# Products of zeros ahead of the first q and k, and a longer placing distance for attention's work on TensorE

## The chip, the cores and the metric

The kernel runs on one core of a Trainium2 chip. The metric is the device time of one execution in microseconds (us). Each kernel was run several times, with runs of the kernel before in between on the same chip. The engines are PE (TensorE; PEld is its weight load), DVE (VectorE), ACT (ScalarE), POOL (GpSimd, which here also issues most loads) and SP (SyncE).

## The reference

Cosine attention for 8 batches, 12 heads, 448 tokens and head size 64, then a mixer: a low-rank sum over tokens (rank 32) and an MLP of 768 to 3072 to 768.

```python
q_n = q / (np.linalg.norm(q, axis=-1, keepdims=True) + 1e-06)
k_n = k / (np.linalg.norm(k, axis=-1, keepdims=True) + 1e-06)
scores = np.matmul(q_n, k_n.transpose(0, 1, 3, 2)) / tau
... softmax ...; x = attn @ v, heads side by side: (8, 448, 768)
h = x.transpose(0, 2, 1) @ U @ V            # sums over tokens
u = x + h.transpose(0, 2, 1)
out = u + np.maximum(u @ w_ch1, 0.0) @ w_ch2
```

## The kernel before

The kernel first writes down all its instructions as entries of a plan, each with an engine, an estimated duration and what it depends on. A small list scheduler then walks through planned time and fixes the order on each engine. On the chip each engine executes its instructions in that order and waits on semaphores where the plan was too optimistic. So the planned times decide only the order.

For PE there are several streams, and at each moment the first stream in the list whose head is ready gets its turn: transposes, then batch 0's scores, then attention times v, then U and V, then scores, and MLP last. MLP products thus fill what attention leaves. When an entry is ready is decided here:

```python
def ready_at(self, op, eng):                       # cut
    for d in op.deps:
        ...
        t = max(t, d.end + self.SEM + (self.SAFE if eng == "PE" else 0.0))   # SEM 0.10, SAFE 0.25
    ...                                             # the same for a buffer that must come free
```

The product of attention's result with U is made of four matmuls, each for 32 columns of the array and with its own token tile; they are four entries of the plan, the last three with a nominal 0.01 us:

```python
for t in range(4):                                  # in stage0, for each range of columns
    o = plan.add(Op("PE", pe_t(c1 - c0) + 0.2 if t == 0 else 0.01,
        lambda ...: nc.tensor.matmul(out=mm.tile[R * t:R * (t + 1), 0:c1 - c0],
            lhsT=U_sb[:, par, t, :], rhs=X.tile[:, t, c0:c1], start=True, stop=True), ...),
        pe_a if c1 < C else pe_av)
```

And batch 0 makes its sums u twice, once more by tokens: six products with V in a row, among the first-layer products of its MLP, each needing one of three PSUM banks that a DVE addition frees:

```python
if b == 0 and f == 9:                               # in mlp, f counts first-layer tiles
    by_tokens(us, *state["first"])                  # six products, six additions
```

## Time and profile before

| | value |
|---|---|
| median time | 607.53 us (607.23 to 608.25, 4 runs) |
| span of the profiled run | 604.8 us |
| PE busy | 586.1 us, 97% |
| first transposes on PE | 7.92 us |
| PE is the limit from | about 32.6 us |

PE's busy share uses modelled ends: a matmul's shown end lies up to 0.16 us behind the moment at which the next could start. Holes are therefore better read from the distance of two starts. Without any wait a score of 448 columns is followed by the next start after 0.189 us, a product of 384 columns after 0.163, one of 512 after 0.216. In this document "excess" is the distance of starts beyond that. The lines of the profile before stand in the prediction. A line of it that begins with two times gives the start (us from the beginning of the span) and the length of a merged run of instructions, then engine, source line, operation, output<-inputs, shapes and count; in brackets stand the engine's idle time before it and what ended that. Line numbers of the changed kernel are mostly two higher than those of the kernel before: scores are L563 and L565, the products with U L640 and L642.

### The profile page before, as it was taken

The page shows a single profiled execution, that of the slowest core. Times are in us where ns is not written, and L with a number is a line of the kernel's source. Part 1 is how long each engine was busy: PE and PEld are TensorE (multiplying, and loading weights), DVE is VectorE, ACT ScalarE, POOL GpSimd, SP SyncE. Part 2 cuts the span into 40 slices and gives each one's busy share as a digit, 9 for nine tenths or more (in the row PEclk, how much of TensorE's full clock was granted, in tenths as well). Part 3 has the DMA queues.
Part 4 walks back from the last instruction along what each step waited for, and adds up shares of the span by engine and source line. Part 5 has one row for each costly group of instructions (what it writes and reads, how often), then busy time and mean ns, then how long its engine had stood idle before and what let it go on. Part 6 is the DMA issues. An engine that isn't in the chain of part 4 may idle for free.

```text
span 604.8 us, 11544 instructions
## 1 busy us (share of the span) xinstructions
PE 586.1 (97%) x4725; PEld 346.8 (57%) x4725; DVE 296.0 (49%) x714; ACT 279.5 (46%) x612; POOL 115.4 (19%) x177
## 2 busy tenths in 40 slices
PE   3899999999999999999999999999999999999997
PEld 1665666555555665666445665666545666654565
DVE  8979679989998987644711253015300210110011
ACT  6977652498782385317641077506442025014300
POOL 8246334071715326000500000000000000000000
PEclk9999999999999999999999999999999999999999
DMA  9999998999999999514902151030002110310021
GB/s 114 202 184 122 208 198 103 173 145 126 129 145 175 151 139 154 83 56 87 154 0 66 46 90 37 1 93 27 15 1 53 52 40 1 92 40 1 0 53 53
DMA packets 150164, 54.58 MB, mean 90 GB/s; under 512 B 115040, under 2 KB 150112, under 8 KB 150112
## 3 DMA queue, kind: packets, MB, share of 16 engines
q0 software_dynamic: 73344, 25.96, 38.6%
q1 hardware_dynamic: 76704, 27.86, 24.2%
q8 instruction: 37, 0.61, 0.4%
q14 instruction: 15, 0.12, 0.1%
q10 hardware_dynamic: 64, 0.02, 0.0%
HBM read 52.25 MB, written 11.01 MB: 105 GB/s over the span
## 4 chain that ended last, share of the span: by engine, by line
PE 92%; ACT 5%; DVE 2%; issue 0%; ACTq 0%
PE mm L785 36%; PE mm L751 35%; PE sc L563 9%; PE av L583 8%; ACT attn L568 3%; PE mm L675 1%; ACT qkT L815 1%; PE tp L365 1%; PE mm L640 1%; DVE ss L452 1%; PE sc L751 1%; DVE xn L527 0%; PE sc L675 0%; ACT uT L815 0%; DVE xn L820 0%
## 5 line engine op out<-in xcount | busy, mean ns | idle before, releaser
L751 PE MATMUL mm<-uT,w_sb 128*128 128x512 bf16 (+1 forms) x1134 | 236.1, 353 | 0.0
L785 PE MATMUL mm<-w_sb,relu 128*128 128x384 bf16 (+1 forms) x1368 | 233.8, 323 | 0.3 <-ACT uT L815 0.3
L568 ACT ACTIVATE attn<-sc 128x448 bf16<-128x448 f32 x336 | 161.0, 565 | 88.8 <-PE av L583 57.4
L785 PEld LDWEIGHTS <-relu 128*128 128x128 bf16 x1368 | 132.6, 98 | 86.7 <-issue 0.9
L751 PEld LDWEIGHTS <-w_sb 128*128 128x128 bf16 x1152 | 111.9, 98 | 101.1 <-issue 1.0
L774 ACT ACTIVATE relu<-mm 128x512 bf16<-128x512 f32 (+1 forms) x169 | 92.4, 547 | 149.2 <-PE mm L751 148.9
L794 DVE TENSOR_TENSOR O_sb<-mm,u_nat 128x384 f32<-128x384 f32 (+1 forms) x57 | 31.0, 547 | 227.1 <-PE mm L785 223.4
L563 PE MATMUL sc<-qkT 128*128 128x448 bf16 x336 | 103.4, 358 | 3.9 <-ACT attn L568 1.9
L583 PEld LDWEIGHTS <-attn 128*128 128x128 bf16 x1536 | 62.7, 98 | 16.0 <-DVE xn L527 0.8
L409 POOL DMA_DIRECT2D v_nat<-in_v_dram x98 | 63.2, 651 | 34.7 <-DMA w_sb<-in_moe_w_ch_dram 13.4
L583 PE MATMUL av<-v_nat,attn 128*128 128x65 bf16 x1536 | 66.6, 194 | 0.2 <-DVE X_sb L592 0.2
L452 DVE TENSOR_REDUCE ss<-sq 112x8 f32<-112x512 bf16 x96 | 63.0, 673 | 0.3
L527 DVE TENSOR_TENSOR xn<-qk_nat,inv 112x512 bf16<-112x512 bf16 (+1 forms) x97 | 62.5, 674 | 0.3
L563 PEld LDWEIGHTS <-qkT 128*128 128x128 bf16 x336 | 29.8, 98 | 24.2 <-issue 8.0
L387 POOL DMA_DIRECT2D qk_nat<-in_q_dram x25 | 17.9, 716 | 130.6 <-DVE xn L527 102.6
L592 DVE TENSOR_TENSOR X_sb<-av,rd 128x256 bf16<-128x256 f32 x96 | 40.0, 419 | 1.5
L590 DVE RECIPROCAL rd<-av 128x4 f32<-128x4 f32 x96 | 17.0, 179 | 38.2 <-PE av L583 36.7
L448 DVE TENSOR_TENSOR sq<-qk_nat 112x512 bf16<-112x512 bf16 x90 | 35.0, 408 | 0.2
L689 DVE TENSOR_TENSOR u_nat<-mm,X_sb 128x384 bf16<-128x384 f32 x36 | 19.1, 553 | 11.0 <-PE mm L675 10.8
L365 PE MATMUL tp<-ident,xn 112*128 112x112 bf16 x144 | 11.7, 226 | 10.0 <-DVE xn L527 9.5
L465 ACT ACTIVATE ln<-ss 112x32 f32<-112x32 f32 (+2 forms) x26 | 6.3, 241 | 32.7 <-DVE ss L452 32.5
L387 POOL DMA_DIRECT2D qk_nat<-in_k_dram x25 | 17.6, 703 | 5.8 <-DMA w_sb<-in_moe_w_ch_dram 5.8
(58 smaller groups left out, 160.8 us busy)
## 6 DMA issues: line engine op xcount, KB each, us to landing
qk_nat<-in_q_dram POOLq DMA_DIRECT2D x23, 224.0 KB, 5.2
qk_nat<-in_k_dram POOLq DMA_DIRECT2D x23, 224.0 KB, 6.4
w_sb<-in_moe_w_ch_dram POOLq DMA_DIRECT2D x4, 1152.0 KB, 14.3
w_sb<-in_moe_w_ch_dram POOLq DMA_DIRECT2D x8, 576.0 KB, 16.6
out_dram<-O_sb SPq DMA_DIRECT2D x15, 168.0 KB, 2.3
out_dram<-O_sb SPq DMA_DIRECT2D x16, 144.0 KB, 2.1
out_dram<-O_sb SPq DMA_DIRECT2D x16, 120.0 KB, 2.0
out_dram<-O_sb SPq DMA_DIRECT2D x16, 96.0 KB, 2.2
```

The lines of the kernel that those rows point to most:

```text
L387: ops = [load(lambda i=i, src=src: nc.gpsimd.dma_start(out=ld.tile[:, i, lo:lo + h1 - h0, :], in_=src[b, h0:h1].rearrange("h (s c) d -> s ...
L409: nc.gpsimd.dma_start(out=vb[p0:p0 + s1 - s0, hs, j, 0:D], in_=v[b, hs].rearrange("h (s c) d -> c s h d", c=SC)[c, s0:s1]),
L448: nc.vector.tensor_mul(y, x, x)
L452: lambda i=i, a0=a0, a1=a1, sq=sq: nc.vector.reduce_sum(ss.tile[:, i, a0:a1, :].rearrange("p h c -> p (h c)"), sq.tile[:, 0:a1 - a0, :].re ...
L527: nc.vector.tensor_mul(dst, src, sc)
L563: nc.tensor.matmul(out=sc.tile[:, 0:S], lhsT=kT[:, 128 * m:128 * (m + 1)], rhs=qkT.tile[:, 8:12, :].rearrange("p c s -> p (c s)"), start=T ...
L568: exps[m] = plan.add(Op("ACT", act_t(S), lambda sc=sc, m=m: nc.scalar.activation(out=attn.tile[:, m, off:off + S], in_=sc.tile[:, 0:S], fu ...
L583: nc.tensor.matmul(out=av.tile[:, t, 0:D + 1], lhsT=attn.tile[:, m, 128 * t:128 * (t + 1)], rhs=v_t[b % 2][:, h, j, 0:D + 1], start=(j == ...
L592: muls.append(plan.add(Op("DVE", dve_t(256), lambda av=av, rd=rd, h=h: nc.vector.tensor_mul(X.tile[:, :, h * D:(h + 1) * D], av.tile[:, :, ...
L751: o = plan.add(Op("PE", pe_t(n), lambda cc=cc: nc.tensor.matmul(out=mm.tile[:, 0:n], lhsT=w1_sb[:, cc, f * 128:(f + 1) * 128], rhs=uT.tile ...
L774: nc.scalar.activation(out=relu.tile[:, f, 0:n], in_=mm.tile[:, 0:n], func=AF.Relu)
L785: nc.tensor.matmul(out=mm.tile[:, 0:c1 - c0], lhsT=relu.tile[:, f, i * 128:(i + 1) * 128], rhs=w2_t[:, f, c0:c1], start=(f == 0), stop=(f ...
```

## The change

It has two parts. Fifty products of zeros run on PE while it waits for the first q and k, with the intent that its clock is already released when the transposes come. And from batch 1 on, the attention entries of PE are placed at a distance of 0.8 us in place of 0.25 behind what they read, so that MLP products go first where the plan was too tight.

```diff
-    SAFE = 0.25
+    safe = 0.25
...
-        op.seq = self.n
+        op.seq, op.safe = self.n, self.safe
...
-                t = max(t, d.end + self.SEM + (self.SAFE if eng == "PE" else 0.0))
+                t = max(t, d.end + self.SEM + (op.safe if eng == "PE" else 0.0))
...
-            t = max(t, f + (self.SEM + self.SAFE if eng == "PE" else self.SEM))
+            t = max(t, f + (self.SEM + op.safe if eng == "PE" else self.SEM))
...
+    warm = const.tile([128, 128], BF, name="warm")
...
+    pe_warm = plan.stream("PE")
...
+    warm_set = fill(lambda: nc.vector.memset(warm, 0.0), 30, prio=-9)
+    hot = Slot(r_mm, 50)
+    for _ in range(50):
+        plan.add(Op("PE", 0.11, lambda: nc.tensor.matmul(
+            out=hot.tile[:, 0:128], lhsT=warm, rhs=warm, start=True, stop=True),
+            deps=[warm_set], acq=[hot], rel=[hot]), pe_warm)
...
     after = last_mul[-1:]
+    plan.safe = 0.8
     state["first"] = prev["A"], prev["X"]
...
+    plan.safe = 0.25
     for b in range(B):
         mlp(b, *state[b])
```

More of the change, by code (lines that the diff above doesn't have):

```diff
@@ L41 @@
 class Op:
-    __slots__ = ("eng", "dur", "fn", "deps", "acq", "rel", "prio", "lat", "start", "end", "by", "seq", "fast")
+    __slots__ = ("eng", "dur", "fn", "deps", "acq", "rel", "prio", "lat", "start", "end", "by", "seq", "fast", "safe")
     def __init__(self, eng, dur, fn, deps=(), acq=(), rel=(), prio=0, lat=0.0, fast=False):
```

## The prediction

> **What bounds the kernel now.** I read the busy shares first, then the stretches of the span, then the chain of waits, then single waits on PE in order of time.
>
> The page's busy shares and chain, by engine:
>
> ```profile
> PE 586.1 (97%) x4725; PEld 346.8 (57%) x4725; DVE 296.0 (49%) x714; ACT 279.5 (46%) x612; POOL 115.4 (19%) x177
> ...
> PE 92%; ACT 5%; DVE 2%; issue 0%; ACTq 0%
> ```
>
> PE carries 92% of the chain that ended last. The other 8%, mostly ACT and DVE, must lie where PE is not yet the limit. The table of stretches says where (columns: length, then busy time of PE, PEld, DVE, ACT, POOL):
>
> ```profile
> 8.00:18.70 10.70, 8.73 (x67) 4.99 (x68) 9.91 (x25) 9.08 (x27) 7.08 (x11) 1.00 1.70 157
> 18.70:32.60 13.90, 11.67 (x169) 8.05 (x168) 12.78 (x40) 13.90 (x37) 5.27 (x8) 1.00 1.16 193
> 32.60:40.00 7.40, 7.39 (x111) 5.00 (x111) 5.47 (x16) 5.78 (x14) 3.03 (x5) 1.00 1.18 187
> 40.00:102.00 62.00, 59.90 (x584) 38.45 (x582) 49.77 (x119) 36.44 (x81) 27.17 (x40) 1.00 1.19 163
> 102.00:240.00 138.00, 137.48 (x1246) 81.44 (x1244) 123.84 (x298) 87.25 (x203) 54.24 (x82) 1.00 1.23 148
> ```
>
> From 8 to 18.7 us DVE is busy 93% (9.91 of 10.70). From 18.7 to 32.6 ACT is busy for all of its 13.90. Only from 32.6 us on is PE the limit, and from there the end of the program is PE's stream of work plus whatever holes are in it. The chain in order of time agrees: DVE pieces up to 14.6 us, a PE piece, ACT pieces up to 32.6, then PE.
>
> What PE waits for first, in the list of waits on PE:
>
> ```profile
> PE tp L365 <- DVE xn L527: 9.5, 4, 7.9
> PE sc L563 <- ACT attn L568: 1.9, 5, 0.6
> PE sc L563 <- ACT qkT L815: 0.7, 2, 0.5
> PE sc L563 <- ACT relu L774: 0.6, 1, 0.6
> ```
>
> The 7.9 us are the start: loads, sums of squares, norms, then the first transposes. The products of zeros go into this hole.
>
> **The clock.** The table's clock column says 1.00 everywhere, but the durations contradict it: a 448-column score lasts a median 554 ns (429 to 581) up to 18.7 us and 350 ns after it; a transpose of 112 columns lasts 301 against 212 ns. The trace's clock record has its entry of full speed only from 18.9 us on; what is not recorded is evidently shown as 1.00. The Trainium skill, page "TensorE: Matmul & The Clock Gate", Part 1, says that PE starts at half clock, that about 3.4 us of sustained activity releases it, and that a start-to-start distance is N/1.2 ns cold and N/2.4 + 2.5 ns warm. The trace agrees: cold scores start 0.36 to 0.37 us apart (17.48, 17.84, 18.21; N/1.2 gives 0.373), warm ones 0.19. Sparse work from 7.9 us on did not release it for 11 us.
>
> **The change, first part: a memset and 50 products.** The same page gives 128/1.2 = 107 ns for each product cold: 50 x 0.107 = 5.35 us, less if the clock is released on the way. The memset of the zeros goes first on DVE, whose first instruction starts at 0.92 us, so the products run from about 1.2 to at most 6.7 us, before the first transposes at 7.92. They hold one of three mm banks until then and collide with nothing. That is 5.4 us of PE work that costs nothing.
>
> The memset does cost a little. DVE is in memsets without a break from 2.19 us to the first squares at 4.88, which its last memset holds up. The page "VectorE: DVE Perf Modes", section "Zero memsets can be issued as uint32 (trn2)", says that a memset takes a cycle per element and that zeros can go as uint32; the trace shows it (xn: 112x512 uint32 in 0.48 us). The zeros are 64 such words per partition: by 36 words in 0.09 and 198 in 0.22, some 0.1 us. It delays the first squares by that: +0.1 us.
>
> What a warm PE saves before 18.9 us counts only where another engine then waits for PE. ACT's waits on PE between 9 and 20 us, in order of time:
>
> ```profile
> 9.75 1.22 ACT L815 COPY qkT<-tp 128x336 bf16<-128x336 bf16 x6 [0.17 <-PE tp L365]
> ...
> 15.57 1.03 ACT L815 COPY qkT<-tp 128x672 bf16<-128x672 bf16 x3 [0.33 <-PE tp L365]
> ...
> 18.08 1.42 ACT L568 ACTIVATE attn<-sc 128x448 bf16<-128x448 f32 x3 [0.46 <-PE sc L563]
> ```
>
> That sums to 0.96 us. Most isn't passed on: the gain of 0.17 and 0.33 meets squares at 16.87 that wait for q and k to land (16.79), and DVE, nearly full, still delivers its normalised tiles at 13.87 and 19.39. I count the 0.46 at 18.08, less a third for DVE's pace: -0.3. PE's own 3.45 us on the chain from 14.61 to 18.05 would shrink by half, but this is the same saving. Net of the memset: -0.2 us, if the clock stays released across the sparse stretch. The page's Part 4 says that transposes don't count as activity in the same way, and the products end over 3 us before the scores at 10.35; I give 65% that it stays.
>
> **The second part: distance 0.25 to 0.8.** The instructions of PE are ordered by a plan made when the program is built; it lets an attention instruction of PE be placed only after its input's planned end plus 0.10 plus this distance. Nothing is added or removed on the chip: MLP products move ahead of attention's by 0.55 us of planned time. What it can gain is the holes after 40 us in which PE, though MLP products were to be had, stood before an attention instruction. The page's idle time hides part of each hole, since the modelled end of a matmul reaches 0.16 us past the next one's possible start. Read from starts: three scores take 0.73 us when nothing waits, four 0.92.
>
> ```profile
> 47.98 0.54 PE L563 MATMUL sc<-qkT 128*128 128x448 bf16 x2 [0.46 <-ACT qkT L815]
> ...
> 58.96 0.54 PE L563 MATMUL sc<-qkT 128*128 128x448 bf16 x2 [0.58 <-ACT relu L774]
> ...
> 147.09 1.10 PE L563 MATMUL sc<-qkT 128*128 128x448 bf16 x3
> ...
> 181.22 1.42 PE L563 MATMUL sc<-qkT 128*128 128x448 bf16 x4
> ...
> 288.95 1.28 PE L563 MATMUL sc<-qkT 128*128 128x448 bf16 x3
> ```
>
> The sum: first scores after qkT copies 0.62 and 0.74; transposes at 77.25 0.31; scores that wait for a bank from the exponentials 0.10, 0.37, 0.50, 0.42 (at 226.6) and 0.55: together 3.6 us. The transposes of u and what follows, 98.9 to 101.05: 0.49 + 0.24 + 0.15 + 0.45 = 1.3. In all 4.9 us. All start-to-start excess after 40 us is 8.7; the rest is mostly the L640 products at every change of column group (0.2 each, some 12 times) and batch 0, which this distance doesn't touch. Single holes are 0.1 to 0.74, so 0.55 more would close them wholly or all but 0.2. I count 75% of the 3.6 (-2.7), 30% of the 1.3 (-0.4; its last part is an MLP product waiting for a bank, and MLP keeps 0.25), and +0.6 for new holes that a new order makes. Net -2.5.
>
> The end is safe: attention's last score starts at 426.4 us and from 430 on PE is without holes for 174 us of MLP, so later attention costs nothing there.
>
> Sum: 607.3 - 0.2 - 2.5 = 604.6; I take 604.5.
>
> **Rivals.** (1) Nothing: the holes move, since a wait was real and the new order waits elsewhere; the clock saves nothing, as ACT and DVE set the pace to 32.6. For it: ACT's full 13.90. Time 606.5 to 607.5. (2) Attention becomes the bound: three score banks with 0.55 us more on each turn are planned at about 0.63 us a score instead of 0.44, so MLP of a batch runs out before the next batch is ready. Against it: batch 4's 42 scores now take 22.7 us (267.9 to 290.6), 26.5 would do, and 130 first-layer products (28 us) of the running batch still lie behind it at 293.6; after batch 1, 72 second-layer products (11.9 us at 101.05) were in hand. For it: DVE is 90% busy from 102 to 240 (123.84 of 138). If it happens: 609 to 612. (3) Warm PE pulls the whole start forward, all 0.96 of ACT's waits, and every hole closes: 607.3 - 0.9 - 4.9 = 601.5.
>
> **Range and chances.** The largest gain worked out is 5.8 us, 1.0%; 2% is 12.1 us. So faster by over 2% needs something not in the profile (1%); slower by over 2% needs a starved PE (1%). The range runs from most holes closed, 602.0, to a slight gain lost in new holes, 606.8.
>
> **What would show it.** Right: scores at 300 to 350 ns instead of 554 before 18.9 us; ACT's waits of 0.33 and 0.46 gone, yet the time at which PE becomes the limit (now 32.6) earlier by under 0.5; the holes at the first scores of a batch and between scores below 0.2; excess after 40 us near 6 instead of 8.7. Wrong: that moment a microsecond or more earlier; new waits of PE on DVE or on u and uT between 90 and 300 us; scores still cold at 12 us.

## The result, and the profile after

The changed kernel took 606.24 us (605.35 to 606.55, 4 runs) against 607.53: ratio 0.9975, 95% interval 0.9957 to 0.9992. Ratios here and below are the mean time of one kernel's fast runs over that of the other's in the same rounds, so they aren't quite the ratio of the medians. In later rounds it took 605.28 against 606.77, ratio 0.9971. So the change wins about 1.5 us, a quarter of a per cent.

The page after, PE's busy line and the chain by engine:

```profile
PE 591.2 (98%) x4775; PEld 351.6 (58%) x4775; DVE 300.7 (50%) x723; ACT 277.7 (46%) x604; POOL 115.7 (19%) x177
...
PE 93%; ACT 3%; DVE 2%; POOL 1%; DMA 1%; issue 0%; ACTq 0%; POOLq 0%
```

The 50 additional instructions are the products of zeros. In the chain (ACTq and POOLq are the sequencers of these engines) POOL and DMA are new: in this run its start goes through loads. PE's waits, longest first:

```profile
PE tp L367 <- DVE xn L529: 3.9, 4, 2.2
PE sc L565 <- ACT attn L570: 1.7, 4, 0.6
PE mm L864 <- DVE warm L861: 1.0, 1, 1.0
PE tp L367 <- ACT qkT L817: 0.4, 1, 0.4
PE sc L565 <- ACT qkT L817: 0.3, 1, 0.3
```

The hole at the start is partly filled (9.5 became 3.9). Of the waits of scores, 0.7 us on the copies of qkT became 0.3, and the 0.6 us on a relu (L774 before) is gone. The table of stretches of the changed kernel (length; then busy PE, PEld, DVE, ACT, POOL with counts; granted clock; DMA share; GB/s):

```profile
5.00:8.00 3.00, 0.85 (x16) 0.67 (x14) 2.90 (x8) 1.29 (x5) 2.92 (x6) 1.00 1.19 145
8.00:18.70 10.70, 8.48 (x66) 4.85 (x66) 9.69 (x25) 8.88 (x26) 7.04 (x11) 0.52 1.71 159
18.70:32.60 13.90, 11.61 (x169) 8.04 (x168) 12.91 (x39) 13.90 (x38) 6.58 (x9) 1.00 1.22 202
```

The clock column of the second row is the surprise: 0.52 from 8 to 18.7 us. The trace's clock record shows full speed from 4.78 us, for 3.41 us, then half speed from 8.20 for 10.24 us, and full again from 18.43. (In all traces here such stretches are whole multiples of 3.41 us, except the last one of a run, which the trace cuts off; this unit is called a window below.) The products (first line below, start 1.0 to 5.5 us, 311 ns cold and 219 warm) did release the clock, but it was gone again before the first scores. Those are as slow as before (second line, the ten up to 18.7 us; before 429 to 581 with a median of 554, eleven of them):

```profile
L864 PE MATMUL mm<-warm x50: 219/311/312, 1.0 to 5.5; 128*128 128x128 bf16 x50
```

```profile
L565 PE MATMUL sc<-qkT x10: 373/544/581, 10.3 to 18.4; 128*128 128x448 bf16 x10
```

**Where the 1.25 us between the two profiled runs come from.** I took the trace's PE instructions in order and summed their excess. Up to 45 us PE had lost 19.86 us before and 20.02 after: +0.16. From 45 us to the last product it lost 7.40 before and 6.19 after: -1.21. The tail after the last product is 4.00 and 3.80. Sorted by kind, the excess over 0.04 us after 40 us, apart from the products with U, fell from 5.54 to 3.08 us:

| excess after 40 us, before what and released by whom | before | after |
|---|---|---|
| scores, by exponentials | 1.94 | 0.49 |
| first scores, by qkT copies or a relu | 1.41 | below 0.1 |
| transposes of u and the product after them | 1.33 | 0.11 |
| by-token products of batch 0 and the product after them | 0.47 | 1.58 |
| products with V, and attention times v | 0 | 0.42 |
| the first MLP products, by batch 0's own uT | 0.40 | 0.40 |

The first scores of batch 1, behind a hole of 0.62 us before (47.98 us in the prediction), now follow the product ahead of them without a wait:

```profile
50.51 0.73 PE L565 MATMUL sc<-qkT 128*128 128x448 bf16 x3
```

And of the four scores that took 1.42 us at 181.22 us in the kernel before, with two holes of about 0.25, the first two now have MLP products between them, and none of the four waits:

```profile
187.98 0.35 PE L565 MATMUL sc<-qkT 128*128 128x448 bf16 x1
188.16 1.14 PE L787 MATMUL mm<-w_sb,relu 128*128 128x384 bf16 x6
189.14 0.35 PE L565 MATMUL sc<-qkT 128*128 128x448 bf16 x1
```

The by-token row is the largest new hole. The products of the changed kernel in order of time:

```profile
49.50 1.17 PE L723 MATMUL mm<-A_sb,V_sb 128*128 128x384 bf16 x3
...
51.87 0.79 PE L723 MATMUL mm<-A_sb,V_sb 128*128 128x384 bf16 x2 [0.24 <-DVE u_nat L727]
...
53.40 0.81 PE L753 MATMUL mm<-uT,w_sb 128*128 128x384 bf16 x4 [0.19 <-DVE u_nat L727]
```

Three such products take 0.65 us without a wait (two distances of 0.163 and one length of 0.32); the first line shows 1.17. Before, scores stood in three of the five gaps between the six, now in two, and most of them wait for a bank.

And there is a loss in the products with U that I hadn't looked for. Before the change (first fence) and after it (second):

```profile
129.78 0.38 PE L751 MATMUL mm<-uT,w_sb 128*128 128x512 bf16 x1
130.09 0.35 PE L640 MATMUL mm<-X_sb,U_sb 128*32 128x384 bf16 x4
130.37 0.36 PE L563 MATMUL sc<-qkT 128*128 128x448 bf16 x1
```

```profile
134.39 0.34 PE L642 MATMUL mm<-X_sb,U_sb 128*32 128x384 bf16 x1
134.66 0.68 PE L585 MATMUL av<-v_nat,attn 128*128 128x65 bf16 x16
135.27 0.34 PE L642 MATMUL mm<-X_sb,U_sb 128*32 128x384 bf16 x3
135.54 0.74 PE L565 MATMUL sc<-qkT 128*128 128x448 bf16 x3
```

Four of them together hold PE for 130.37 - 130.09 = 0.28 us, and the first starts 0.31 us after the 512-column product before it, 0.09 later than that one's pace of 0.216. They use different columns of the array and run side by side, as the Trainium skill says in "TensorE: Matmul & The Clock Gate", Part 3 ("Packing small matmuls"). Split in one and three, each part holds PE for 0.27 us (134.66 - 134.39 and 135.54 - 135.27) and each pays the 0.09 in front. One split of this size so costs about 0.27 + 0.09 = 0.36 us, as much as a whole group. The changed kernel has four such splits after 40 us (at 78, 88, 134 and 169 us, of different widths), the kernel before none; both have one in batch 0.

The excess at these groups grew by 1.17 us. In the kernel before it still held a hole right behind one group, which the change closed: the transposes at 77.25 us start 0.54 us after that group's first product (76.71), and a whole group of 512 columns holds PE for 0.33 (from 34.01 to 34.34 us in the kernel whole4 below), so the hole is 0.21 us. The splits themselves so cost 1.17 + 0.21, about 1.4 us. Holes closed by 2.46 + 0.21 = 2.7 us, splits opened 1.4: net 1.3, which is the result.

### The profile page after: what moved, and what is told of

The parts are those of the page before. It is cut to its first block, busy times and chain, and to the rows that moved or that the text cites. A ratio compares the mean times of both kernels' runs of the same rounds, so it can differ in the third digit from the quotient of the medians.

```text
span 603.6 us, 11632 instructions
## 1 busy us (share of the span) xinstructions
PE 591.2 (98%) x4775; PEld 351.6 (58%) x4775; DVE 300.7 (50%) x723; ACT 277.7 (46%) x604; POOL 115.7 (19%) x177
## 4 chain that ended last, share of the span: by engine, by line
PE 93%; ACT 3%; DVE 2%; POOL 1%; DMA 1%; issue 0%; ACTq 0%; POOLq 0%
PE mm L787 36%; PE mm L753 35%; PE sc L565 10%; PE av L585 8%; ACT attn L570 2%; PE mm L677 1%; DMA v_nat<-in_v_dram 1%; PE mm L642 1%; PE tp L367 1%; POOL v_nat L422 1%; POOL qk_nat L389 1%; PE sc L753 0%; ACT qkT L817 0%; DVE xn L529 0%; DVE ss L454 0%
## 5 line engine op out<-in xcount | busy, mean ns | idle before, releaser
L753 PE MATMUL mm<-uT,w_sb 128*128 128x512 bf16 (+1 forms) x1134 | 239.4, 353 | 0.2 <-DVE u_nat L727 0.2
L570 ACT ACTIVATE attn<-sc 128x448 bf16<-128x448 f32 x336 | 164.1, 560 | 105.5 <-PE av L585 52.6
L776 ACT ACTIVATE relu<-mm 128x512 bf16<-128x512 f32 (+1 forms) x158 | 86.6, 548 | 129.8 <-PE mm L753 129.1
L565 PE MATMUL sc<-qkT 128*128 128x448 bf16 x336 | 101.6, 358 | 2.3 <-ACT attn L570 1.7
L565 PEld LDWEIGHTS <-qkT 128*128 128x128 bf16 x336 | 28.5, 98 | 21.1 <-issue 7.1
L778 DVE TENSOR_SCALAR relu<-mm 128x384 bf16<-128x384 f32 (+1 forms) x31 | 18.7, 605 | 12.6 <-PE mm L753 11.9
```

The lines of the kernel that those rows point to most:

```text
L565: nc.tensor.matmul(out=sc.tile[:, 0:S], lhsT=kT[:, 128 * m:128 * (m + 1)], rhs=qkT.tile[:, 8:12, :].rearrange("p c s -> p (c s)"), start=T ...
L570: exps[m] = plan.add(Op("ACT", act_t(S), lambda sc=sc, m=m: nc.scalar.activation(out=attn.tile[:, m, off:off + S], in_=sc.tile[:, 0:S], fu ...
L753: o = plan.add(Op("PE", pe_t(n), lambda cc=cc: nc.tensor.matmul(out=mm.tile[:, 0:n], lhsT=w1_sb[:, cc, f * 128:(f + 1) * 128], rhs=uT.tile ...
L776: nc.scalar.activation(out=relu.tile[:, f, 0:n], in_=mm.tile[:, 0:n], func=AF.Relu)
```

## The experiments

The theory after reading the two traces: (a) the products of zeros give nothing; (b) the distance closes some 2.5 us of holes; (c) its new order splits groups with U, which gives back 1.2 (so I counted it at the time; the 0.21 behind a group was found later). The rivals: (A) the products won the time; (B) the splits are harmless; (C) a full clock would pay if it only lasted; and, for a longer distance, the prediction's rival of a starved PE. All kernels gave correct results.

| kernel | median us (runs) | ratio to before, 95% |
|---|---|---|
| changed kernel, first rounds | 606.24 (4) | 0.9975 (0.9957 to 0.9992) |
| warm_only | 607.41 (5) | 1.0007 (0.9995 to 1.0020) |
| dist_only | 605.64 (5) | 0.9981 (0.9968 to 0.9993) |
| whole4 | 603.27 (5) | 0.9945 (0.9933 to 0.9958) |
| fill | 605.73 (5) | 0.9979 (0.9965 to 0.9992) |
| fill512 | 604.79 (5) | 0.9963 (0.9950 to 0.9975) |
| whole4_cold | 604.09 (5) | 0.9944 (0.9932 to 0.9957) |
| before_whole4 | 605.91 (5) | 0.9981 (0.9968 to 0.9993) |
| spread_cold | 603.08 (5) | 0.9932 (0.9917 to 0.9946) |
| after_again (changed kernel) | 605.28 (5) | 0.9971 (0.9958 to 0.9983) |
| whole4_late | 604.14 (5) | 0.9952 (0.9940 to 0.9965) |
| start512 | 603.33 (5) | 0.9941 (0.9928 to 0.9953) |
| spread_16 | 620.69 (5) | 1.0224 (1.0210 to 1.0238) |

Rows two to five share their rounds (before: 606.81), the next four (607.03) and the last four (606.77).

### Each part alone

**warm_only**: the changed kernel with the distance left at 0.25. The order of PE's other instructions is exactly that of the kernel before.

```diff
-    plan.safe = 0.8
+    plan.safe = 0.25
```

> The 50 products and their memset alone; distance 0.25 everywhere, and the other PE instructions in the order of the kernel before. Theory: the clock is released one window (3.4 us) only and is back at half before the first scores, so nothing is gained: ratio to before 0.9995 to 1.0005 (-0.3 to +0.3 us), the 448-column scores up to 18 us stay near 550 ns. Rival A: the products are what won the measured 1.3 us: -0.8 to -1.5 us, ratio about 0.998.

Measured: ratio 1.0007, and the lost time of PE up to 45 us is 20.19 us against 19.86. The products give nothing; rival A falls. Whether they cost 0.3 us (that profile) or nothing is within the scatter. One part of the theory missed: in this profile the clock was full for two windows, from 3.81 to 10.63 us, and the first two scores took 363 and 353 ns, yet nothing was won.

**dist_only**: the changed kernel without the products, their memset and their stream. PE's order is exactly that of the changed kernel.

> The distance of 0.8 alone, no products; the PE order is that of the changed kernel. Theory: all of the gain is here: -1.0 to -1.6 us (ratio 0.9974 to 0.9984), first-layer products of batch 0 reach full pace at 40.6 us as before. Rival A (products did it): within 0.4 us of before.

Measured: ratio 0.9981, 1.2 us less than before, with PE's loss up to 45 us at 19.86, as before. The gain is the distance's alone.

### The split groups

**whole4**: the four products with U become one entry of the plan.

```diff
-            for t in range(4):
-                o = plan.add(Op("PE", pe_t(c1 - c0) + 0.2 if t == 0 else 0.01,
-                                lambda t=t, ...: nc.tensor.matmul(...),
-                    deps=... if t == 0 else (), acq=[mm, A] if t == 0 else []), ...)
+            o = plan.add(Op("PE", pe_t(c1 - c0) + 0.23,
+                            lambda ...: [nc.tensor.matmul(...) for t in range(4)],
+                deps=need + consts[:2 + par], acq=[mm, A]), ...)
```

> The changed kernel with the four products with U of a column range made one entry of the plan, so that nothing is placed between them. In the changed kernel's trace four such groups after 40 us are split by other products (before: none), and the sum of PE's excess there is 1.2 us worse on just these. Theory: the splits cost 0.3 us each, so this is 1.2 us faster than the changed kernel: -2.2 to -2.8 us against before (ratio 0.9953 to 0.9963). Rival B: the splits are harmless and the excess moves elsewhere: equal to the changed kernel, -1.0 to -1.6 us.

Measured: 603.27 us, ratio 0.9945, 3.3 us less than before and more than the theory's 2.2 to 2.8. PE's loss up to 45 us is 19.37 us against the changed kernel's 20.02, so up to 0.65 us of it may belong to batch 0's own group, which is also whole here; single profiles of the start scatter by more than that (see whole4_late), so this share is not shown. The rest had to be separated:

**whole4_late**: the same for batches 1 to 7 only; batch 0 stays split, and PE's order is the changed kernel's up to its 704th product.

```diff
-            for t in range(4):
+            for t in range(4) if b == 0 else ():
...
+            if b:
+                o = plan.add(Op(... the one entry of whole4 ...))
```

> The changed kernel with the products with U kept together in batches 1 to 7 only; batch 0 keeps its split, and the order of PE is the changed kernel's up to its 704th instruction outside the products of zeros. Theory: the four splits that the longer distance made cost 1.2 us: -0.9 to -1.4 us against the changed kernel of the same rounds, with the loss before 45 us unchanged. Rival B: within 0.4 us of it.

**after_again**, the changed kernel in the same rounds:

> The changed kernel itself once more, unaltered, as the reference of these rounds. Expected as before: -1.0 to -1.8 us against the kernel before (ratio 0.997 to 0.9984).

Measured: 604.14 against 605.28 us, 1.14 us less, within the 0.9 to 1.4 that the theory gave. In the profile the group that had been split stands whole:

```profile
134.38 0.35 PE L649 MATMUL mm<-X_sb,U_sb 128*32 128x384 bf16 x4
134.66 0.68 PE L585 MATMUL av<-v_nat,attn 128*128 128x65 bf16 x16
```

From 45 us on this profile loses 1.3 us less than the changed kernel's, 1.2 of it at the groups with U. That settles (c). One part of the expectation missed: the loss up to 45 us was not unchanged but 20.84 us in the profiled run. That run was the slowest of the five (604.66), and its first v load landed at 12.79 us where the changed kernel's landed at 12.18, so I take this for the scatter of loads.

**before_whole4**: the kernel before with whole groups.

> The kernel before (distance 0.25, no products) with the four products with U kept together. It has one split, in batch 0, at 33.8 and 35.3 us. whole4 reached full-pace first-layer products of batch 0 0.86 us before the changed kernel. Theory: that part of whole4's gain is batch 0's split and comes here too: -0.5 to -1.0 us against before (ratio 0.9984 to 0.9992), and nothing more after 40 us. If whole4's early gain came from elsewhere: 0 +- 0.3.

Measured: ratio 0.9981, 1.15 us. That is a little more than expected for batch 0's one split, and not only the start: in the profile the start was even slower (20.35 us lost up to 45 us, with v landing at 12.92), while the loss after 45 us fell from 7.40 to 6.82. A new order has moved some holes too, so this kernel doesn't isolate the start. It does show that whole groups help without any of the change.

**whole4_cold**: whole4 without the products.

> whole4 without the products and their memset; PE's order otherwise the same. Theory: they give nothing and delay DVE by 0.1 us: -0.4 to +0.2 us against whole4. If they help by what the prediction gave them (0.2) or by rival A: +0.2 to +1.0.

Measured: ratio 0.9944 against 0.9945, the same. A second time, with the same order of PE otherwise, the products are worth nothing that shows. This kernel also isolates the distance: it differs from before_whole4, of the same rounds, in nothing else. It is faster by 1.8 us by the medians, 2.2 by the means and by the ratios. So the distance wins about 2 us where it can't split a group, and 1.2 (dist_only) where it does.

### Would a clock that lasts pay?

**fill**: whole4 with more products, 89 at the start and 43 in the plan's gaps of PE up to about 17 us.

```diff
+    for n_, dur_ in [(60, 0.09)] + [(12, 0.06)] * 6:
+        hot = Slot(r_mm, n_)
+        for _ in range(n_):
+            plan.add(Op("PE", dur_, ... the same product of zeros ...))
```

> whole4 with 132 products of zeros in place of 50: 89 at the start (to about 7.8 us) and the others in the plan's gaps of PE up to about 17 us, so that the clock stays full. Theory: scores fall to 350 ns from 10 us on, but ACT and DVE set the pace to 32 us: 0.0 to -0.4 us against whole4, and the first-layer products of batch 0 reach full pace at 40.2 to 40.6 us. Rival C: the cold clock is what holds the start back: -0.8 to -1.5 us against whole4, with that point at 39.1 to 39.8 us.

Measured: the clock was full from 4.34 to 21.41 us, all scores in that stretch took 349 to 353 ns, and yet the kernel was 2 us slower than whole4; both theories missed. The chain of waits of this profile runs through loads (start, length, what):

```profile
5.96 8.08 DMA v_nat<-in_v_dram
...
14.32 4.17 DMA qk_nat<-in_q_dram
```

The first v load lands at 14.04 us; in the thirteen other profiles it is 11.66 to 13.06. POOL issues the next q load only after it (14.32 us, against 12.47 in the kernel before), and ACT and DVE wait for that q.

**fill512**: the same filling by 33 products of 512 columns.

> As fill (clock kept full from 4.5 us on), but with 33 products of 512 columns in place of 132 of 128: the same work of PE in a quarter of the instructions. In fill's trace a 16 KB packet of instructions was fetched at 11.3 us, none before 16 us in the other runs, and the first v load landed at 14.04 us (else 11.7 to 12.5), which held back the next q load by 1.9 us. Theory: the extra instructions did it: here v lands at 11.7 to 12.7 us, the last q of batch 0 at 16.5 to 17.5, scores at 350 ns from 10 us on, and the time is within 0.5 us of whole4, since a fast PE gains nothing while q, DVE and ACT set the pace. Rival D: a busy PE, or the order that the fill changes, did it: v again at 13.5 us or later and +1.5 to +2.5 us against whole4. Rival C of before (cold clock holds the start back): -0.8 to -1.5 us against whole4.

Measured: v landed at 12.45 us and q at 17.56, and the first seven scores took 349 to 353 ns; the clock was full from 5.12 to 15.36 us. So a busy PE in itself didn't delay v here. In fill one 16 KB packet of instructions was fetched at 11.3 us; here the first came at 20.0, and no other run had one before 19. That fits the instructions as the cause, but no run isolates it. The time missed the expectation, though: ratio 0.9963 against 0.9945, about 1.1 us slower than whole4. This plan orders PE differently from its 30th product on. The profile has a hole of 0.82 us at the transposes of u which whole4 hasn't, and 0.44 us more excess at the groups with U, so fill512 doesn't decide about the clock.

**start512** keeps whole4's order to the last product: 24 products of 512 columns take the place of the 50.

```diff
-            out=hot.tile[:, 0:128], lhsT=warm, rhs=warm, ...
+            out=hot.tile.rearrange("p (a n) -> p a n", a=4), lhsT=warm,
+            rhs=warm.unsqueeze(1).to_broadcast([128, 4, 128]), ...    # 24 of the 50 entries; the others issue nothing
```

> whole4 with 24 products of 512 columns in place of 50 of 128, to about 7.8 us, and the rest of PE's order exactly that of whole4, which fill and fill512 did not keep. Theory: clock full from about 4.5 to 11 us or later, so the first scores take 350 ns, and yet the time is whole4's within 0.5 us (ratio 0.9938 to 0.9955), the waits of ACT on PE being replaced by waits on DVE and on q. Rival C: a full clock at the first scores is worth 0.8 us or more against whole4 (ratio below 0.9935).

Measured: 603.33 us, ratio 0.9941, no different from whole4. The clock was full from 5.52 to 12.35 us. The first line is of the scores up to 12.3 us; the next two are ACT in order of time:

```profile
L565 PE MATMUL sc<-qkT x4: 349/352/363, 10.3 to 12.1; 128*128 128x448 bf16 x4
```

```profile
15.59 1.03 ACT L816 COPY qkT<-tp 128x672 bf16<-128x672 bf16 x3 [0.34 <-PE tp L367]
...
17.97 0.63 ACT L448 ACTIVATE sq<-qk_nat 112x512 bf16<-112x512 bf16 x1 [1.23 <-DMA qk_nat<-in_q_dram]
```

The first four scores run at full speed and nothing comes of it. ACT starts its first exponentials at 11.43 and 11.96 us, where the changed kernel, with cold scores, starts them at 11.41 and 11.94, and later it still waits, now 1.23 us for q. The kernel before had no such wait, only 0.15 us before the same squares at 16.87. For the scores up to 12 us rival C falls. A full clock all the way from 8 to 19 us with undisturbed loads and whole4's order was not reached by any run, so for the transposes and products between 14 and 18 us it stays open.

### The holes that remain, and a still longer distance

**spread_cold**: whole4_cold with the by-token products one by one.

```diff
-            if b == 0 and f == 9:
-                by_tokens(us, *state["first"])
+            if b == 0 and 9 <= f < 21 and f % 2:
+                by_tokens(us, *state["first"], (f - 9) // 2)     # one of the six
```

> whole4_cold with the six products of batch 0's by-token sums placed one to every second first-layer tile (from the tenth) in place of six in a row: with the longer distance no scores fill between them any more, and PE waits there for banks that DVE's sums free (in whole4 1.85 us in all, between 49 and 54 us). Expected if those holes close: -1.0 to -1.8 us against whole4_cold, -4.2 to -5.2 against before (ratio 0.9915 to 0.993). If they reopen elsewhere, since DVE is full there: 0 to -0.5.

Measured: 603.08 against 604.09 us, the medians 1.0 us apart, and ratio 0.9932; the lower end of the expected gain by the medians, just short of it by the ratios (0.0012 of 607 is 0.7). In the profile the 1.75 us of holes around these products are gone (the expectation's 1.85 for whole4 is 1.64 at these products and 0.21 at 193.8 us, in a later batch); 0.75 us reopen at first-layer products that wait for relus on ACT, and products with V wait 0.6 us more for DVE. This is the fastest kernel, 0.7% less than before; its margin over whole4_cold is within the two intervals.

**spread_16**: the same with the distance at 1.6.

> spread_cold with the distance at 1.6 in place of 0.8. Theory: the holes that wait for exponentials, 0.34 us left in spread_cold, are already closed, and a later attention costs nothing while MLP products are in hand: -0.4 to +0.6 us against spread_cold (ratio to before 0.9925 to 0.994). Prediction's rival of a starved PE, if it exists at all, shows here: +2 us or more.

Measured: 620.69 us, 2.2% slower than before and 17.6 us slower than spread_cold. The expectation missed: the rival that I had called unlikely exists, only further out. Some of PE's waits in this kernel (L674 is products with V, L639 with U), and then the stretch from 110 to 135 us of spread_16 and, last, of spread_cold:

```profile
PE sc L674 <- ACT attn L568: 2.7, 2, 2.5
...
PE sc L674 <- DVE u_nat L688: 2.1, 3, 1.4
PE sc L639 <- DVE X_sb L592: 1.8, 1, 1.8
```

```profile
110.00:135.00 25.00, 15.18 (x114) 8.38 (x111) 24.63 (x61) 9.98 (x24) 10.81 (x17) 0.73 1.11 133
```

```profile
110.00:135.00 25.00, 25.00 (x220) 13.55 (x218) 23.26 (x57) 18.76 (x44) 11.00 (x17) 1.00 1.12 144
```

Batch 1's attention isn't done when batch 0's MLP has run out at about 110 us. Then PE has nothing to put between: it waits in single steps on DVE (24.63 of 25 us busy) and ACT, and makes 114 products where spread_cold makes 220. It also loses the clock, 0.73 on average. From 100 to 150 us it loses 17.2 us (41.42 - 24.27), spread_cold 0.95. No run tried a distance other than 0.25, 0.8 and 1.6, so where between them the best one lies, and how much of the gain is peculiar to the one order that 0.8 makes, stays open.

## Why the prediction was right or wrong

Predicted 604.5 us, a range of 602.0 to 606.8 and "within 2%" at 98%; measured 606.24. The range held and the direction was right, but the gain was half of what was predicted: 1.3 to 1.5 us against 2.8.

- **What bounds the kernel.** Right. PE's stream from about 32 us on sets the end, and the start is set by other engines. One refinement: in the changed kernel's first profile the chain's start runs through v and q loads rather than through DVE; in its second (after_again) it runs through DVE again. The two are close, and the scatter of loads seems to decide.
- **First part, that the clock stays (65%).** Wrong. It fell back after one window of 3.41 us, at 8.20, before the first scores. When it falls differs by the run: with the same products it was full from 6.90 to 10.31 us in after_again and from 3.81 to 10.63 in warm_only, in both gone again among the first scores. That transposes count less as activity, which the prediction took from Part 4 of the skill's page, no run isolates. The prediction's own sign of being wrong, scores still cold at 12 us, came true (the four from 12.05 us on took 530 to 533 ns). The next step, that a faster PE would hardly matter there, was right: start512 had fast first scores and gained nothing. The net of -0.2 us was predicted; warm_only and whole4_cold show 0, within 0.4.
- **The memset's 0.1 us.** The zeros went as 64 words per partition, as "VectorE: DVE Perf Modes", section "Zero memsets can be issued as uint32 (trn2)", has it, and took 0.11 us. DVE's first squares started at 4.96 in place of 4.88. By the first normalised tile the 0.1 was gone again (7.15 against 7.17).
- **Second part, holes closed.** Right in sum: net -2.5 predicted, -2.7 in the traces without the splits (-2.2 by the pair before_whole4 and whole4_cold). The pieces differ. Scores and qkT closed by about 3 us, 2.7 counted (one of the holes read there, the 0.31 at 77.25, is 0.21). The transposes of u closed nearly wholly, 1.2 us in place of 0.4. New holes were 1.5 us in place of 0.6, most of them at the by-token products of batch 0, which I had noted as untouched by the distance. They aren't: they keep 0.25, but the scores that used to stand between them have moved.
- **The failed step** is "Nothing is added or removed on the chip: MLP products move ahead of attention's". Its term for the cost of a new order was +0.6 us. An order is not free where neighbours share the array: four groups with U were split, at 0.25 to 0.41 us each by their width and 1.4 us in all. whole4_late, which only undoes that, is 1.14 us faster than the changed kernel, and so 2.6 us under the kernel before of its rounds, near the predicted 2.8. With the 1.5 us of new holes the new order cost 2.9 us in place of 0.6, while the holes that closed were 4.2 us in place of 3.1. That the second miss hid part of the first is luck. The excess after 40 us so fell from 8.7 to 7.4, where the prediction's sign of being right was near 6.
- **Rival 2, the starved PE.** Rightly put aside at 0.8, but with too much confidence in the margin: at 1.6 it costs 17.6 us. The prediction named two margins, 28 us of products in hand behind batch 4's scores and 11.9 us at 101 us, after batch 1; the stream ran dry at the smaller one. Its reading of batch 4 is also off: by count the trace's 42 scores from 176.1 to 220.6 us are batch 4's, and those around 270 to 293 us belong to batches 5 and 6.

## What to carry to other kernels

A list scheduler that reorders for waits will also cut apart products that the hardware runs side by side; tie such a group into one entry before tuning distances, and compare groups as well as waits afterwards. A safety distance helps only while there is other work to put in front: look for the stage with the least work in hand, since the step from 0.8 to 1.6 cost 17.6 us, where the step from 0.25 to 0.8 had won about 2. Before warming an engine's clock, check in the trace that it is still warm when the work arrives, and that somebody waits for that engine there.

## What the Trainium skill lacked or had wrong

- "TensorE: Matmul & The Clock Gate", Part 1, has in its table that the clock falls back after at least one idle window of about 3.4 us; its section on a second failure mode also tells of a kernel in which short idle times were enough. Here it fell back at the end of windows that weren't idle. In the changed kernel the window from 4.78 to 8.20 us held the last products until 5.7 and four transposes; in start512 the clock fell at 12.35 us, though PE was busy 2.44 of the 4.30 us from 8.0 to 12.3; in spread_16 it was at half for 10.24 us from 124.3 on, while PE was waiting in steps of up to 2.5 us. How much activity holds it isn't on the page. The lengths agree with the page: full or half lasted, for example, 3.41, 6.83, 10.24, 13.65 or 17.07 us, whole windows.
- The same page, Part 3, gives the gain of running products in different columns side by side, but not what it costs to come between them; "TensorEngine Tiling (Array Packing)", section "Key Properties", has only that a change of tiling mode drains TensorE, without a time. Here it is about 0.36 us for each interruption of a group of four (0.27 for the second part and 0.09 in front of it), while the whole group takes 0.28.
- "Runtime: NRT & Kernel Launch", section "Instruction fetch mechanics", describes the fetch of instructions in blocks of 16 KiB and calls its cost mostly hidden; no page says whether a fetch can hold back a kernel's loads. Here such packets take about 0.9 us or more each. In fill one came at 11.3 us and v landed at 14.04, 1.0 to 2.4 us later than elsewhere; in the others none of this size came before 19 us. That the one caused the other isn't shown.
